# Loading one weight matrix in pieces over interleaved partitions, and the output in two stores

## The chip, the core and the metric

The kernel runs on one NeuronCore of a Trainium2 chip. The metric is the device time of one execution in microseconds (us). A profile of one execution shows what each engine did: TensorE (PE, with its weight loads PEld), VectorE (DVE), ScalarE (ACT), GpSimd (POOL), SyncE (SP, which issues most DMAs), and 16 DMA engines that all DMAs share.

## The reference

Two attention branches, A and B, take the same x (2 batches, one new token, 512 features). Each projects x to 32 heads of 128, attends over a cache of 4096 keys and values per head, and multiplies the result by output weights `wo` of 4096 x 512. A sigmoid gate mixes the branches. All is float32.

```python
g = sigmoid((x * gate_w).sum(-1, keepdims=True))
def branch(x, k, v, wq, wo):                      # k, v: (2, 32, 4096, 128)
    q = (x @ wq) as (2, 32, 1, 128)
    p = softmax(q @ k^T * 128 ** -0.5)
    return (p @ v) as (2, 1, 4096) @ wo
out = g * branch(A) + (1 - g) * branch(B)         # (2, 1, 512)
```

## The kernel before

The caches are read once, 512 MB of them, in 32 units: a unit is four heads of one batch of one branch (A's 16 units first, then B's). A K or V tile of a unit is 128 partitions x 64 KB: partition 32h + s holds positions 128s to 128s + 127 of head h of the four. Three buffers of 64 KB per partition carry all the large tiles: two named `kt` (K tiles, the query weights, the last unit's V and B's output weights) and one named `vt` (V tiles, and A's output weights at the end).

Per unit, `scores` (L158, L159) multiplies K by the query on VectorE and sums over the head dimension; `soft` (L164 to L172) finds the maximum on VectorE and takes the exponentials on ScalarE; `values` (L184) multiplies the probabilities with V on TensorE. The program order is written out by hand. All large loads are issued by SP and so wait in one queue: `load_k` (L65), `load_v` (L72), `load_wq` (L76), `load_wo` (L82 for A, L86 for B). A load that reuses a buffer waits at SP until the last reader of the buffer is done, and what SP issues later waits behind it.

At the end of the loop, unit 30 issues the last V (into a `kt` buffer) before its `values`, and A's output weights after it, since they take over the `vt` buffer that `values` reads. Unit 31 issues B's output weights after its scores are done. A's weights, 32 blocks of 512 columns per partition (64 KB, `NJ` = 32), come in one DMA over 128 partitions. B's come in six over 128 partitions, of 16, 8, 4, 2, 1 and 1 blocks (`TAIL`).

After the loop, `finish("B")` normalizes B's rows. TensorE then adds A's 32 and B's first 24 blocks into four strips of one PSUM tile (L252), ScalarE copies it (L255), four matmuls add up the strips (L259), and B's last eight blocks are added as they arrive (L262). VectorE copies the sum to `res` (L265), in which partition 32s + b holds columns 128s to 128s + 127 of batch b. Four stores of 2 partitions x 512 B write it out (L269), two issued by SP and two by ScalarE (ACT).

The small inputs, x (2 rows) and `gate_w` (1 row), are loaded by ScalarE's queue at the start (L90, L91).

Of the kernel before, what the change touches and what calls it, by code (L numbers as in the profile page):

```python
# [13 lines left out]
P = 128  # L14
B = 2
H = 32
SK = 4096
DH = 128
D = 512
KC = D // P  # L20
QP = 32
# [4 lines left out]
STRIPS = P // QP  # L26
HG = H // HU
HP = 2 * HU
NJ = D * H * DH // (P * D)
NB = 24  # L30
TAIL = ((0, 16), (16, 24), (24, 28), (28, 30), (30, 31), (31, 32))
PRW = QP + HU
# [5 lines left out]
def tile_gated_decode(ctx: ExitStack, tc: tile.TileContext, ins: dict, out: bass.AP):  # L38
    nc = tc.nc
# [12 lines left out]
    kt, vt, wq, wo = {}, {}, {}, {}  # L52
# [25 lines left out]
    def load_wo(n):  # L78
        src = ins[n + "_wo"].rearrange("(p j) e -> p j e", j=NJ)
        if n == "A":  # L80
            wo[n] = big.tile([P, NJ, D], F32, name="vt", bufs=1)
            nc.sync.dma_start(wo[n], src)  # L82
        else:
            wo[n] = big.tile([P, NJ, D], F32, name="kt")
            for i, j in TAIL:
                nc.sync.dma_start(wo[n][:, i:j], src[:, i:j])  # L86
# [63 lines left out]
    gat, rows = {}, {}  # L150
# [57 lines left out]
    def finish(n):  # L208
# [4 lines left out]
        nc.vector.tensor_tensor(r, r, rl[:, 1, :, None].to_broadcast([H, B, DH]), op=ALU.mult)  # L213
        t = ps.tile([P, B, NJ], F32, name="small")
        for q in range(HU):
            nc.tensor.matmul(t, deal[:, HU - 1 - q:HU - 1 - q + P], r[:, :, q * NJ:(q + 1) * NJ],  # L216
                             start=q == 0, stop=q == HU - 1)
        on[n] = work.tile([P, NJ, B], F32, name="on")
        nc.vector.tensor_copy(on[n].rearrange("p j b -> p b j"), t)
# [4 lines left out]
    for u in range(NU):  # L224
        scores(u)
        soft(u)
        if u == per_branch:
            finish("A")
        if u == per_branch - 2:
            load_wq("B")  # L230
        elif u == NU - 2:
            load_v(NU - 1)
        elif u == NU - 1:
            load_wo("B")
        else:
            load_k(u + 2 if u != per_branch - 1 else per_branch)
            if u == per_branch - 1:
                project("B")
                load_k(per_branch + 1)
        values(u)  # L240
        if u == NU - 2:
            load_wo("A")
        elif u < NU - 2:
            load_v(u + 1)
# [4 lines left out]
    for n in "AB":  # L249
        for j in range(NJ if n == "A" else NB):  # L250
            s = j % STRIPS
            nc.tensor.matmul(bulk[s * QP:s * QP + B], on[n][:, j], wo[n][:, j],  # L252
                             start=n == "A" and j < STRIPS, stop=n == "B" and j >= NB - STRIPS)
    bs = work.tile([P, D], F32, name="vs", bufs=1)
# [3 lines left out]
    for s in range(STRIPS):  # L258
        nc.tensor.matmul(acc[s * QP:s * QP + B], strip[:, :B], bs[:, s * DH:(s + 1) * DH], start=True, stop=False)  # L259
    for j in range(NB, NJ):  # L260
        for s in range(STRIPS):
            nc.tensor.matmul(acc[s * QP:s * QP + B], on["B"][:, j], wo["B"][:, j, s * DH:(s + 1) * DH],  # L262
                             start=False, stop=j == NJ - 1)
    res = consts.tile([P, DH], F32)
    nc.vector.tensor_copy(res, acc)  # L265
    dst = out.rearrange("b s e -> (b s) e")
    for s in range(STRIPS):
        eng = nc.sync if s % 2 == 0 else nc.scalar
        eng.dma_start(dst[:, s * DH:(s + 1) * DH], res[s * QP:s * QP + B])  # L269


# [20 lines left out]
```

## Time and profile before

| what | us |
|---|---|
| median of 3 runs | 1327.87 (1327.73 to 1327.96) |
| the profiled execution, whole | 1328.29 |
| its span, from the first to the last instruction | 1326.5 |
| VectorE busy | 1129.2 (85% of the span) |
| TensorE matmuls busy | 365.3 (28%) |
| ScalarE busy | 81.5 (6%) |

The mean granted TensorE clock of this execution was 0.645.

How to read the lines that follow. The queues of the page give packets, megabytes and the share of the 16 DMA engines' time; q1 is SP's queue, q10 ScalarE's, q8 and q14 bring instruction code. The chain is followed back from the last instruction to what released each step; in order of time it gives start, duration and what it was. The timeline gives start, duration, engine, line, operation, output<-input and count, with the idle time before in brackets and what ended it. The view by windows gives for a stretch, after its length, the busy time of PE, PEld, DVE, ACT and POOL with counts, then the granted clock, the mean busy share of the DMA engines and the GB/s they moved. A wait line gives who waited for what, the sum in us, how often, and the longest. A line's own view gives minimum, median and maximum duration in ns, and the first and last start in us.

### The profile page before, as it was taken

To read this page: it belongs to the slowest core of one execution; us is meant where nothing else is said; L and a number is where in the kernel's file an instruction comes from. 1 tells how busy PE (TensorE), PEld (TensorE's weight loads), DVE (VectorE), ACT (ScalarE), POOL (GpSimd) and SP (SyncE) were. 2 spreads that over 40 slices of the span, in tenths; PEclk is the share of its full clock that TensorE was granted. 3 is DMA by queue.
4 is the path that set the end of the run, shared out by engine and by line. 5 is a ranking of instruction groups with operands and counts; after the bars stand their busy time and mean duration, and the time that the engine had idled before them with its cause. 6 is when DMAs were issued, how large, how long until landed. Compare 5 with 4: busy or idle time off the path is not lost.

```text
span 1326.5 us, 5935 instructions
## 1 busy us (share of the span) xinstructions
PE 365.3 (28%) x2582; PEld 102.9 (8%) x2582; DVE 1129.2 (85%) x187; ACT 81.5 (6%) x283; POOL 1.8 (0%) x8
## 2 busy tenths in 40 slices
PE   3123113232321222231532122323212232320255
PEld 1000000000000000000111000000000000000011
DVE  1999988889988888998269999889888888988850
ACT  0000000000000000000000000000001000000000
POOL 0000000000000000000000000000000000000000
PEclk9666566666656666665865566666556666655678
DMA  9999999999999999999999999999999999999997
GB/s 411 441 413 441 441 435 423 437 441 419 441 435 439 425 439 431 437 433 427 433 440 435 433 435 428 441 435 429 431 441 437 425 435 439 437 421 439 441 432 317
DMA packets 10848, 570.82 MB, mean 430 GB/s; under 512 B 1211, under 2 KB 1219, under 8 KB 1606
## 3 DMA queue, kind: packets, MB, share of 16 engines
q1 hardware_dynamic: 10808, 570.43, 99.4%
q8 instruction: 20, 0.33, 0.1%
q14 instruction: 6, 0.05, 0.0%
q10 hardware_dynamic: 14, 0.01, 0.0%
HBM read 570.43 MB, written 0.00 MB: 430 GB/s over the span
## 4 chain that ended last, share of the span: by engine, by line
DVE 50%; DMA 49%; issue 0%; PE 0%; SPq 0%; DVEq 0%
DVE sc L159 25%; DVE kt L158 25%; DMA kt<-in_A_k_cache_dram 25%; DMA kt<-in_B_k_cache_dram 22%; DMA kt<-in_B_wo_dram 3%; PE small L216 0%; SPq L86 0%; DVE rm L164 0%; DVE tm L166 0%; DVE nm L168 0%; PE q L262 0%; DVE rows L213 0%; SPq L76 0%; DVEq L159 0%; DVE res L265 0%
## 5 line engine op out<-in xcount | busy, mean ns | idle before, releaser
L158 DVE TENSOR_TENSOR kt<-kt,q 128x16384 f32<-128x16384 f32 (+1 forms) x34 | 551.3, 16215 | 133.3 <-DMA kt<-in_B_k_cache_dram 71.8
L159 DVE TENSOR_REDUCE sc<-kt 128x128 f32<-128x16384 f32 (+1 forms) x34 | 551.3, 16216 | 3.2
L184 PE MATMUL vp<-vt,pr 128*32 128x512 f32 x1984 | 283.6, 736 | 856.6 <-DMA vt<-in_A_v_cache_dram 446.0
L184 PEld LDWEIGHTS vp<-vt,pr 128*32 128x32 f32 x1984 | 78.5, 132 | 1059.7 <-issue 1059.7
L172 ACT ACTIVATE pr<-sc,nm 32x128 f32<-32x128 f32 x128 | 66.2, 517 | 755.2 <-DVE nm L168 752.4
L144 PE MATMUL q<-kt,xb 128*32 128x512 f32 x256 | 30.8, 642 | 22.5 <-DMA kt<-in_B_wq_dram 12.0
L189 ACT ACTIVATE vs<-vp 128x512 f32<-128x512 f32 x16 | 9.6, 597 | 440.8 <-PE vp L184 440.8
L172 ACT ACTIVATION_READ_ACCUMULATOR pr<-sc,nm 32x1 f32 x128 | 25.2, 197 | 0.0
L193 PE MATMUL gat<-vs,strip 128*32 128x512 f32 x32 | 16.7, 605 | 11.4 <-ACT vs L189 11.4
L265 DVE COPY res<-q 128x128 f32<-128x128 f32 x1 | 0.3, 292 | 22.6 <-PE q L262 22.6
L210 DVE RECIPROCAL rl<-rows 32x2 f32<-32x2 f32 x2 | 0.3, 148 | 17.3 <-ACT rows L206 17.3
L216 PE MATMUL small<-rows,deal 32*128 32x64 f32 x16 | 3.0, 346 | 35.0 <-DVE rows L213 35.0
L184 PE MATMUL vp<-kt,pr 128*32 128x512 f32 x64 | 9.6, 770 | 10.4 <-DMA kt<-in_B_v_cache_dram 10.4
L144 PEld LDWEIGHTS q<-kt,xb 128*32 128x32 f32 x256 | 8.6, 118 | 43.9 <-issue 33.3
L164 DVE TENSOR_REDUCE rm<-sc 128x1 f32<-128x128 f32 x32 | 9.2, 286 | 1.1
L252 PE MATMUL q<-vt,on 128*2 128x512 f32 x64 | 8.5, 691 | 3.8 <-DMA vt<-in_A_wo_dram 3.8
L166 DVE STREAM_TRANSPOSE tm<-rm 128x32 f32<-128x32 f32 x32 | 6.8, 212 | 1.1
L118 DVE COPY xg<-small 128x12 f32<-128x12 f32 x1 | 0.2, 171 | 8.3 <-PE small L116 8.3
L168 DVE TENSOR_REDUCE nm<-tm 128x1 f32<-128x32 f32 x32 | 6.0, 186 | 1.1
L252 PE MATMUL q<-kt,on 128*2 128x512 f32 x48 | 5.5, 592 | 2.3 <-DMA kt<-in_B_wo_dram 2.3
L216 PEld LDWEIGHTS small<-rows,deal 32*128 32x128 f32 x16 | 2.7, 254 | 35.5 <-ACT pr L172 34.0
L203 PE MATMUL small<-vs,pick 128*32 128x128 f32 x32 | 4.2, 276 | 2.8 <-ACT vs L199 2.8
(44 smaller groups left out, 30.4 us busy)
## 6 DMA issues: line engine op xcount, KB each, us to landing
kt<-in_A_k_cache_dram SPq DMA_DIRECT2D x2, 4096.0 KB, 36.2
kt<-in_B_k_cache_dram SPq DMA_DIRECT2D x2, 4096.0 KB
kt<-in_B_wo_dram SPq DMA_DIRECT2D x1, 4096.0 KB
kt<-in_B_wo_dram SPq DMA_DIRECT2D x1, 2048.0 KB
kt<-in_B_wo_dram SPq DMA_DIRECT2D x1, 1024.0 KB, 39.8
kt<-in_B_wo_dram SPq DMA_DIRECT2D x1, 512.0 KB
kt<-in_B_wo_dram SPq DMA_DIRECT2D x2, 256.0 KB, 40.8
vt<-in_A_v_cache_dram SPq DMA_DIRECT2D x16, 29.3
```

The source lines that it names most:

```text
L144: nc.tensor.matmul(q[h * QP:(h + 1) * QP], xb[:, b, c, :], cols[:, c, h, half * HG // 2:(half + 1) * HG // 2, :], start=c == 0, stop=c == ...
L158: nc.vector.tensor_tensor(k, k, q[:, None, :].to_broadcast([P, j - i, DH]), op=ALU.mult)
L159: nc.vector.tensor_reduce(sc[u][:, i:j], k, axis=AX.X, op=ALU.add)
L164: nc.vector.tensor_reduce(rm[:, 0:1], sc[u], axis=AX.X, op=ALU.max)
L166: nc.vector.transpose(tm, rm[:, 0:1].to_broadcast([P, QP]))
L168: nc.vector.tensor_reduce(nm, tm, axis=AX.X, op=ALU.max, negate=True)
L172: nc.scalar.activation(w, sc[u][r].rearrange("p (c a) -> p c a", a=VC), AF.Exp, bias=nm[r], accum_out=lsum[r, g * HU + h:g * HU + h + 1])
L184: nc.tensor.matmul(o[s * QP:(s + 1) * QP], pr[:, c, at:at + QP], vt[u][:, c * VC:(c + 1) * VC, :].rearrange("p a d -> p (a d)"), start=not ...
L189: nc.scalar.activation(vs, o, AF.Copy)
L193: nc.tensor.matmul(gat[n, b][r:r + QP], strip, vs, start=True, stop=True)
L216: nc.tensor.matmul(t, deal[:, HU - 1 - q:HU - 1 - q + P], r[:, :, q * NJ:(q + 1) * NJ], start=q == 0, stop=q == HU - 1)
L252: nc.tensor.matmul(bulk[s * QP:s * QP + B], on[n][:, j], wo[n][:, j], start=n == "A" and j < STRIPS, stop=n == "B" and j >= NB - STRIPS)
```

## The change

A's output weights come in six DMAs, all issued by SP in the same place: blocks 0 to 7 over all 128 partitions, then blocks 8 to 31 (48 KB per partition) in five DMAs that each take some of the partitions: 0, 2, 4, ... (64 of them); 1, 5, 9, ... (32); 3, 11, 19, ... (16); 7, 15, ..., 63 (8); 71, 79, ..., 127 (8). Together they load what the one DMA loaded. The output is written by two stores, one of each batch's four pieces of 512 B, the first issued by SP and the second by ScalarE.

```diff
+NA = 8
...
         if n == "A":
             wo[n] = big.tile([P, NJ, D], F32, name="vt", bufs=1)
-            nc.sync.dma_start(wo[n], src)
+            nc.sync.dma_start(wo[n][:, :NA], src[:, :NA])
+            for rows in (slice(0, P, 2), slice(1, P, 4), slice(3, P, 8), slice(7, P // 2, 8), slice(P // 2 + 7, P, 8)):
+                nc.sync.dma_start(wo[n][rows, NA:], src[rows, NA:])
...
-    dst = out.rearrange("b s e -> (b s) e")
-    for s in range(STRIPS):
-        eng = nc.sync if s % 2 == 0 else nc.scalar
-        eng.dma_start(dst[:, s * DH:(s + 1) * DH], res[s * QP:s * QP + B])
+    dst = out.rearrange("b o (s e) -> b (o s) e", s=STRIPS)
+    src = res.rearrange("(s q) e -> q s e", q=QP)
+    nc.sync.dma_start(dst[0], src[0])
+    nc.scalar.dma_start(dst[1], src[1])
```

## The prediction

> **What bounds the kernel now.** I read the page first: queues, HBM rate and chain.
>
> ```profile
> span 1326.5 us, 5935 instructions
> q1 hardware_dynamic: 10808, 570.43, 99.4%
> q8 instruction: 20, 0.33, 0.1%
> q14 instruction: 6, 0.05, 0.0%
> q10 hardware_dynamic: 14, 0.01, 0.0%
> HBM read 570.43 MB, written 0.00 MB: 430 GB/s over the span
> DVE 50%; DMA 49%; issue 0%; PE 0%; SPq 0%; DVEq 0%
> ```
>
> The chain passes through VectorE and the DMAs in equal shares, but the busy DMA share of each stretch (second-last column of the view by windows) says which of the two waits for the other:
>
> ```profile
> 140.00:600.00 460.00, 118.61 (x790) 32.18 (x790) 420.69 (x57) 27.76 (x98) 0.00 (x0) 0.62 1.00 434
> 600.00:1280.00 680.00, 181.51 (x1260) 51.80 (x1260) 598.71 (x95) 42.04 (x149) 0.00 (x0) 0.64 1.00 433
> ```
>
> For 1140 us the engines of the DMA are never idle, at 434 and 433 GB/s. The bytes at that rate are the time; VectorE, 420.69 of 460 us busy, keeps up. The change moves the same bytes, so only the end counts. There I read the chain in order of time and the timeline:
>
> ```profile
> 1281.16 40.83 DMA kt<-in_B_wo_dram
> 1322.04 0.44 PE q L262 x8
> 1322.51 0.29 DVE res L265
> ```
>
> ```profile
> 1283.43 9.64 PE L184 MATMUL vp<-kt,pr 128*32 128x512 f32 x64 [10.44 <-DMA kt<-in_B_v_cache_dram]
> 1302.73 8.50 PE L252 MATMUL q<-vt,on 128*2 128x512 f32 x64 [3.82 <-DMA vt<-in_A_wo_dram]
> 1312.31 3.62 PE L252 MATMUL q<-kt,on 128*2 128x512 f32 x32 [1.07 <-DMA kt<-in_B_wo_dram]
> 1317.16 1.90 PE L252 MATMUL q<-kt,on 128*2 128x512 f32 x16 [1.24 <-DMA kt<-in_B_wo_dram]
> 1322.83 0.62 SPq L269 DMA_DIRECT2D out_dram<-res  x2
> 1322.83 0.83 ACTq L269 DMA_DIRECT2D out_dram<-res  x2
> ```
>
> The last V lands at 1283.4, A's output weights (8 MB) at 1302.7, the pieces of B's from 1312.3 on, the last at 1322.04. From there eight matmuls, one copy and the stores lead to the end. How evenly the 16 engines arrive there shows in half-microseconds:
>
> ```profile
> 1317.00:1317.50 0.50, 0.34 (x4) 0.11 (x8) 0.00 (x0) 0.00 (x0) 0.00 (x0) 1.00 0.80 328
> 1317.50:1318.00 0.50, 0.50 (x8) 0.10 (x4) 0.00 (x0) 0.00 (x0) 0.00 (x0) 1.00 0.75 307
> 1318.00:1318.50 0.50, 0.50 (x12) 0.10 (x4) 0.00 (x0) 0.00 (x0) 0.00 (x0) 1.00 0.55 225
> 1318.50:1319.00 0.50, 0.50 (x8) 0.00 (x0) 0.00 (x0) 0.00 (x0) 0.00 (x0) 1.00 0.54 217
> 1319.00:1319.50 0.50, 0.06 (x4) 0.00 (x0) 0.00 (x0) 0.32 (x1) 0.00 (x0) 1.00 0.50 197
> 1319.50:1320.00 0.50, 0.17 (x8) 0.17 (x12) 0.00 (x0) 0.28 (x1) 0.00 (x0) 1.00 0.54 213
> 1320.00:1320.50 0.50, 0.50 (x27) 0.48 (x23) 0.00 (x0) 0.00 (x0) 0.00 (x0) 1.00 0.36 127
> 1321.50:1322.04 0.54, 0.35 (x12) 0.06 (x8) 0.00 (x0) 0.00 (x0) 0.00 (x0) 1.00 0.02 8
> ```
>
> The share stands near one half for two microseconds: eight engines are through early (the last at about 1319.3, by the 0.50), eight late (1320 to 1322.04). Two more things: the rate per share does not rise when half of them are idle (225/0.55 = 409, 213/0.54 = 394 GB/s), so the limit belongs to each engine's own way and is not a pool; and one engine's pace is 433/16 = 27.1 GB/s.
>
> **How rows go to engines.** Queue q10 carries x (2 rows), the gate (1 row) and two stores of 2 rows: 7 data packets, yet it has 14. Queue q1 has 75 loads of 128 rows (34 of K, 32 of V, 2 of the query weights, 7 of the output weights) and two stores: 75 x (128 + 16) + 2 x (2 + 2) = 10808, exactly its count. So each row is a packet, and each engine that takes part adds one: 16 engines for 128 rows, 2 for 2 rows. A load of 8 rows thus runs on eight engines at most.
>
> **The change, part by part.**
>
> 1. Extra rows. 64, 32 and 16 rows give each engine 4 + 2 + 1 = 7 rows of 48 KB where it had 8; the two 8-row loads give 2 more to each of eight engines, if it is the same eight. Eight engines then carry 9 rows and eight carry 7. One row is 49152 B / 27.1 GB/s = 1.8 us. If the early eight get them, the late ones end at 1322.04 - 1.8 = 1320.2 and the early ones at 1319.3 + 1.8 = 1321.1: a gain of 0.9. If the late eight get them: 1.8 lost.
>
> 2. Pace of the small pieces. All 75 loads of before cover all 128 partitions; none of 16 or 8 rows, eight partitions apart, was timed. From below: such a row keeps the 1.8 us (no excess is possible the other way, since 27.1 GB/s is held everywhere). From above: if an engine's way ends in a group of partitions, rows eight apart load some groups from two engines and leave others empty, and each row takes twice as long: x = 1.8 us more. The receiving eight have three such rows (16, 8 and 8), the others one. The nearest row is the rate per share above: every way is full when the rows are spread evenly, and an idle neighbour lends nothing. I take the upper end: a full way that gets a second stream can only halve it. Then the receiving eight, if they are the early ones, end at 1319.3 + 1.8 + 3 x 1.8 = 1326.5, and the others at 1320.2 + 1.8 = 1322.0. Load term: 1326.5 - 1322.04 = +4.5.
>
> [...]
>
> Which eight receive? No view numbers the engines. The rows that bear on it:
>
> ```profile
> 1324.00:1324.50 0.50, 0.00 (x0) 0.00 (x0) 0.00 (x0) 0.00 (x0) 0.00 (x0) 1.00 0.04 17
> 1324.50:1325.00 0.50, 0.00 (x0) 0.00 (x0) 0.00 (x0) 0.00 (x0) 0.00 (x0) 1.00 0.01 2
> q14 instruction: 1, 0.01, 1.1%
> ```
>
> (the last from the DMA view of 1323.4 to 1325.2). The lateness must come from work that only some engines have, and q8's 20 code packets of 0.33 MB are the only such work of size: 2 or 3 each for eight engines, 16.5 KB or 0.6 us apiece at least. The last store traffic (1324.5 on) comes just after a q14 packet of 8 KB, as if stores of two rows shared engines with q14, which leaves q8 to the others. An 8-row load uses the engines of a 2-row transfer and six more, I assume. From this alone I put it at a little over 8 in 10 that the receiving eight are the early ones.
>
> [...]
>
> 3. More packets and waits: +0.1. Each engine has 15 or 17 rows for A's weights instead of 8, and 6 or 4 completion packets for one. B's last small pieces, 2 to 8 KB a row, ran at 394 to 409 GB/s per share against 433, up to 9% below; at 16 and 48 KB I take a tenth of that, under 1% of the 19.3 us of this load, with bounds of 0 and 0.5.
>
> 4. Issues and queues on SP.
>
> ```profile
> SPq L82 <- PE vp L184: 9.4, 1, 9.4
> SPq L86 <- DVE rm L164: 5.8, 1, 5.8
> SPq L269 <- DMA vt<-in_A_wo_dram: 21.0, 1, 21.0
> ```
>
> ```profile
> 1273.04 0.33 SPq L82 DMA_DIRECT2D vt<-in_A_wo_dram  x1
> 1278.90 2.70 SPq L86 DMA_DIRECT2D kt<-in_B_wo_dram  x6
> ```
>
> ```profile
> L252 PEldq EVENT_SEMAPHORE  x1: 51/51/51, 1302.6 to 1302.6; - x1
> ```
>
> A's load is issued at 1273.04, when the reader of V's buffer is done (the 9.4 us). Five more issues at 2.70/6 = 0.45 take 2.3 us and end at 1275.7. SP then waits for B's buffer until 1278.90 (the 5.8 us), which covers them; uncovered they would cost nothing either, as the last V still streams until 1283.4. The 21.0 us at L269 is a store that waits for A's weights although it doesn't use them: issues inherit the semaphore of one some eight earlier. With five loads put between, B's second piece will wait for V's landing (1283.4), and its third to sixth for A's first four pieces: 1288.2 (2 MB at 433), 1295.5, 1299.1, 1300.9. Behind the waiting SP stand only these pieces and the stores. Engines want the third piece at 1317.2, the early eight some 4 us sooner; 12 us of cover, cost 0. PE waits for six loads instead of one: five more waits of 51 ns, before 1302.7 and hidden. A's matmuls can start on the first quarter; 48 are left after the landing, 6.4 us instead of 8.50, so even a landing 4.5 later is done by 1313.6, ahead of B's first piece, which is later too. Cost 0.
>
> 5. The stores.
>
> ```profile
> L269 SPq DMA_DIRECT2D out_dram<-res x2: 257/289/321, 1322.8 to 1323.2; - x2
> L269 ACTq DMA_DIRECT2D out_dram<-res x2: 253/253/253, 1322.8 to 1323.4; - x2
> SPq L288 <- DMA out_dram<-res: 1.9, 1, 1.9
> ```
>
> Each queue issues one instead of two; the second started 0.4 (SP) and 0.6 (ACT) after the first. Those go for certain if landing takes as long: 0.4 is the lower end. The first pair's traffic is over by 1324.0, the second's falls after 1324.5; with the wait of 1.9 us for the last landing the upper end is 1.5. A store of 4 pieces of 512 B instead of 2 costs no more, on more engines. I take -0.9, nearer the middle, since the code packet may still be in the way.
>
> Sum: +4.5 + 0.1 - 0.9 = +3.7. The profiled execution took 1328.29 (1.8 around its span), 0.4 over the median of 1327.87: 1332.0 there, **1331.6** as a median.
>
> **The rivals.**
> - A: the small pieces keep their pace and the early eight get the rows: -0.9 + 0.1 - 0.9 = -1.7, **1326.2**; up to -1.8 + 0 - 1.5 = -3.3 if the early eight are done by 1318.4. Its point: with an excess x per row the sum is -1.7 + 3x, so under 0.6 us a row the change is not slower. For it: no narrow load is slow in any row. Against: idle ways lend nothing.
> - B: the late eight get the rows. With doubling 1322.04 + 1.8 + 5.4, +7.2 + 0.1 - 0.9 = +6.4, **1334.3**; without, +1.0. For it: no view numbers engines; against: the q14 packet among the stores.
> - C: the pieces are taken to overlap, as their partitions interleave, and each waits for the one before. Four waits of 0.45 (issue) plus some 0.7 (the stores are issued at 1322.83, traffic from 1323.5) add 4.6 with everything idle, and each 8-row load leaves eight engines idle for 1.8 us: +4.6 + 1.8 - 0.9, **1333.4**. For it: SP does inherit waits here; against: the partitions are disjoint.
> - D: the change does not shift anything, the two 8-row loads falling to different eights. Eight rows each; two of them doubled: +3.6 + 0.1 - 0.9, **1330.7**; without doubling 1327.1.
>
> **How the numbers follow.** Forecast 0.52, A 0.23, B 0.14, C 0.05, D 0.06. A measurement of this kernel tells about 0.2% from no change, 2.7 us: bounds 1325.2 and 1330.5. Faster: half of A, 0.12. Slower: of the forecast 0.44, the rest having x of 1.4 or less, B 0.12, C 0.05, D 0.03: 0.64. Same 0.24. The range runs from 1325.2 (A's better half left out) to 1335.2, B with its doubling inside; 0.17 is left out.
>
> **What would show it.** In the windows of 1290 to 1310, GB/s clearly under 420 with the DMA share still near 1 (doubled rows), or unchanged (A). At the end, a plateau of 0.5 that is later and ends later (forecast), gone (A), or twice as long (B). B's last landing at 1326.5, 1321.1 or 1329. Waits of SP at the line of A's pieces show C. The stores: one each, the end less than 3.9 us after the copy. The forecast is wrong above all if narrow loads keep 27.1 GB/s per engine.

## The result and the profile after

The changed kernel takes **1337.29 us** (median of 6 runs, 1335.37 to 1337.96); before, on the same chip, 1327.72 (6 runs, 1327.67 to 1327.96). The ratio is 1.0068, 95% interval 1.0058 to 1.0078: slower by 9.6 us where 3.7 were forecast, and above the range. The profiled execution took 1337.33.

The page after, span, queue and rate:

```profile
span 1335.5 us, 5939 instructions
q1 hardware_dynamic: 11000, 570.43, 99.3%
HBM read 570.43 MB, written 0.00 MB: 427 GB/s over the span
```

The bytes are the same; 192 packets more are 128 rows and 64 completion packets (4 x 16 + 2 x 8 for the six loads, less 16), so, at one completion packet an engine as counted in the prediction, the 8-row loads do run on eight engines each. The timeline after, in the order of time (line numbers are 3 higher than before):

```profile
1272.15 3.19 SPq L85 DMA_DIRECT2D vt<-in_A_wo_dram  x5
1298.84 3.59 PE L255 MATMUL q<-vt,on 128*2 128x512 f32 x16 [0.91 <-DVE q L251]
1312.76 7.56 PE L255 MATMUL q<-vt,on 128*2 128x512 f32 x48 [10.33 <-DMA vt<-in_A_wo_dram]
1321.95 3.61 PE L255 MATMUL q<-kt,on 128*2 128x512 f32 x32 [1.63 <-DMA kt<-in_B_wo_dram]
1326.80 1.90 PE L255 MATMUL q<-kt,on 128*2 128x512 f32 x16 [1.23 <-DMA kt<-in_B_wo_dram]
1331.69 0.40 PE L265 MATMUL q<-kt,on 128*2 128x128 f32 x8 [0.23 <-DMA kt<-in_B_wo_dram]
1332.16 0.29 DVE L268 COPY res<-q 128x128 f32<-128x128 f32 x1 [33.24 <-PE q L265]
1332.48 0.58 SPq L271 DMA_DIRECT2D out_dram<-res  x1
1332.49 0.63 ACTq L272 DMA_DIRECT2D out_dram<-res  x1
```

All of A's weights are there at 1312.76 instead of 1302.73, ten microseconds later, and every later piece stays that late: B's last lands at 1331.69 instead of 1322.04, +9.65. From there to the end it takes 3.81 us (1335.5 - 1331.69) instead of 4.46. So the whole loss arises before 1312.76 and it is one of loading. Where in that time, the windows of 5 us tell (last three columns: granted clock, DMA share, GB/s; a packet counts whole in the stretch in which it begins, so a share can pass 1). Before:

```profile
1293.00:1298.00 5.00, 2.33 (x18) 1.12 (x14) 0.72 (x3) 1.46 (x3) 0.00 (x0) 1.00 0.94 403
1298.00:1303.00 5.00, 1.18 (x12) 0.91 (x15) 0.85 (x3) 0.00 (x0) 0.00 (x0) 0.59 0.96 413
1303.00:1308.00 5.00, 5.00 (x36) 0.93 (x32) 0.00 (x0) 0.00 (x0) 0.00 (x0) 0.73 1.02 439
1308.00:1313.00 5.00, 3.93 (x40) 0.79 (x36) 0.00 (x0) 0.00 (x0) 0.00 (x0) 1.00 0.93 398
```

and after:

```profile
1288.00:1293.00 5.00, 4.29 (x40) 1.08 (x32) 0.00 (x0) 0.60 (x1) 0.00 (x0) 1.00 0.94 406
1293.00:1298.00 5.00, 2.98 (x17) 2.18 (x16) 0.75 (x4) 0.87 (x2) 0.00 (x0) 0.88 1.27 308
1298.00:1303.00 5.00, 3.59 (x16) 0.40 (x16) 0.82 (x3) 0.00 (x0) 0.00 (x0) 0.50 0.95 206
1303.00:1308.00 5.00, 0.00 (x0) 0.00 (x0) 0.00 (x0) 0.00 (x0) 0.00 (x0) 0.50 0.98 252
1308.00:1313.00 5.00, 0.24 (x4) 0.14 (x8) 0.00 (x0) 0.00 (x0) 0.00 (x0) 0.50 0.83 249
1313.00:1318.00 5.00, 5.00 (x28) 0.86 (x24) 0.00 (x0) 0.00 (x0) 0.00 (x0) 0.57 0.94 406
```

Read share and rate together: from 1298 to 1313, for 15 us, the engines are about as busy as before and move 50 to 63% of what they did. Had only the eight engines with doubled rows been slow, the rate would have been three quarters, some 320. Against the 427 of the span the four low windows lack 119, 221, 175 and 178 GB/s; times 5 us and over 427 that is **8.1 us of loading**, or 16 us at half pace. The other 1.5 us are not in them.

### The profile page after: what moved, and what is told of

It is laid out like the page before. It is cut to its first block, busy times and chain, and to the rows that moved or that the text cites. A ratio compares the mean times of both kernels' runs of the same rounds, so it can differ in the third digit from the quotient of the medians.

```text
span 1335.5 us, 5939 instructions
## 1 busy us (share of the span) xinstructions
PE 374.2 (28%) x2582; PEld 104.1 (8%) x2582; DVE 1129.2 (85%) x187; ACT 81.5 (6%) x283; POOL 1.8 (0%) x8
## 4 chain that ended last, share of the span: by engine, by line
DMA 76%; PE 23%; issue 0%; SPq 0%; DVE 0%
DMA vt<-in_A_v_cache_dram 36%; DMA vt<-in_B_v_cache_dram 34%; PE vp L187 22%; DMA vt<-in_A_wo_dram 2%; DMA kt<-in_B_wo_dram 2%; DMA kt<-in_A_wq_dram 2%; PE q L147 1%; SPq L85 0%; PE q L265 0%; SPq L83 0%; SPq L66 0%; DVE res L268 0%
## 5 line engine op out<-in xcount | busy, mean ns | idle before, releaser
L187 PE MATMUL vp<-vt,pr 128*32 128x512 f32 x1984 | 288.5, 746 | 851.1 <-DMA vt<-in_A_v_cache_dram 444.5
L255 PE MATMUL q<-vt,on 128*2 128x512 f32 x64 | 11.2, 858 | 11.2 <-DMA vt<-in_A_wo_dram 10.3
```

Of the source, the lines that this page charges most:

```text
L187: nc.tensor.matmul(o[s * QP:(s + 1) * QP], pr[:, c, at:at + QP], vt[u][:, c * VC:(c + 1) * VC, :].rearrange("p a d -> p (a d)"), start=not ...
```

## The experiments

The theory after this reading, called that of pairs below: two DMA engines whose rows end in one group of partitions halve each other (step 2 of the prediction). A group is the set of partitions that one engine alone writes in a load over all 128; that engine is the group's owner, and another that writes there a guest. That there are such groups, which partitions form one and which engine owns it is my assumption: no view and no packet record numbers the engines. So where I say below, or the expectations, that rows share a group or lie in their engines' own, it is the theory that says so; what the runs show is which rows were loaded, how long they took and at what rate. Its rivals: that the number of DMAs and waits costs; that loads of few rows are slow whatever their partitions; that the uneven rows cost (9 and 7 an engine). And, once the size was known: that one shared group holds up all 16 engines, not only the two that share it. Differences below are of medians, each against before on the same chip (1327.69 to 1327.87).

**The stores alone**, the loads as before.

> The loads of before with the two stores of after. From the start of the last eight matmuls to the end of the span it was 4.46 us before (1326.5 - 1322.04) and 3.81 after (1335.5 - 1331.69), so if the stores alone did that: 0.65 us faster than before, 0.4 to 0.9. If the stores only looked better after because the code packet came at another time, nothing: within 0.2 us of before.

1327.02 against 1327.87, -0.85; ratio 0.9995 (0.9986 to 1.0004), so not told from none by the clock alone. Its trace, page, timeline and waits:

```profile
span 1325.3 us, 5933 instructions
...
1321.60 0.40 PE L262 MATMUL q<-kt,on 128*2 128x128 f32 x8 [0.19 <-DMA kt<-in_B_wo_dram]
...
SPq L288 <- DMA out_dram<-res: 1.1, 1, 1.1
```

From the last matmuls to the end 3.70 us, 0.76 less than before; the wait for the last landing is 1.1 instead of 1.9. Its median is the lowest of all the kernels here, though not told from that of before.

**The loads alone**, with the four stores of before. All the runs that follow have these stores too.

> The six loads of after with the four stores of before. All theories put the loss on the loads and differ only on its kind: the last landing was 9.65 us later after (1331.69 against 1322.04), the stores gave back 0.65, so +9.6 to +10.3 over before. If loads and stores act on each other (other engines taking the stores), it would be off that by over 0.5 us.

1337.55, **+9.68**; ratio 1.0071 (1.0057 to 1.0085). Loads and stores don't act on each other as far as this can tell.

**Other pieces.** Each run changes the list of rows:

```diff
-for rows in (slice(0, P, 2), slice(1, P, 4), slice(3, P, 8), slice(7, P // 2, 8), slice(P // 2 + 7, P, 8)):
+for rows in (slice(0, P, 2), slice(1, P, 4), slice(3, P, 4)):                      # 64, 32, 32
+for rows in (slice(0, P, 2), slice(1, P, 4), slice(3, P, 8), slice(7, P, 8)):      # 64, 32, 16, 16
+for rows in (slice(0, P // 2), slice(P // 2, P)):                                  # halves
+for rows in (slice(0, P, 2), slice(1, P, 2)):                                      # even, odd
```

> The last three pieces (16, 8 and 8 rows, eight apart) made one of 32 rows, four apart; stores of before. Theory (two engines whose rows end in one group of partitions halve each other): 32 rows four apart spread over all groups like the other two pieces, each engine has eight rows, so +0 to +0.5. Rival that the number of DMAs, waits and completion packets costs: three more loads instead of five, so three fifths of some 10 us, +6. Rival that any load of fewer than 128 rows is slow: 56 of 64 KB... the same pieces of 64 and 32 rows and a third, +5 or more.

> The two loads of 8 rows made one of 16 rows, eight apart; stores of before. No engine has more rows than another. Theory of shared groups: two rows of every engine take twice the time, +3.6 if the pace of the others is not touched; after lost 10 with a forecast of 4.5 for its loads, so by the same ratio +8. Rival that the nine rows of eight engines make the loss (the imbalance): +0 to +0.5.

> Two pieces of 64 rows instead of the five: partitions 0 to 63, then 64 to 127; stores of before. Wide pieces, eight rows for each engine, but all 16 engines on one half of the partitions at a time. Theory of shared groups, if a group is a block of neighbouring partitions or of partitions eight apart within a half: every row of 48 KB takes twice the time as long as all engines are in the same piece, 8 x 1.8 = +14.4 at most, +7 or more. If groups cut across both halves, or if only pieces of few rows are slow: +0 to +0.5.

> As the run with two halves, but partitions 0, 2, 4, ... and then 1, 3, 5, ...; stores of before. The 64 rows two apart kept the pace in after, so +0 to +0.5 by every theory but one: that a load of fewer than 128 rows is slow whatever its partitions, which gives this run the time of the one with halves.

| pieces | us | against before | ratio (95%) |
|---|---|---|---|
| 64, 32, 32 | 1328.13 | +0.26 | 1.0005 (0.9996 to 1.0014) |
| 64, 32, 16, 16 | 1335.71 | +7.84 | 1.0061 (1.0046 to 1.0077) |
| halves | 1347.68 | +19.88 | 1.0147 (1.0132 to 1.0162) |
| even, odd | 1328.13 | +0.33 | 1.0004 (0.9995 to 1.0013) |

64 rows cost nothing that can be told two apart and 19.9 us side by side, over the 14.4 that I had as the most. It isn't the width of a load but which partitions it has. The windows of the run by halves, the first, one in the middle, and the last of the eight low ones, and the first after them:

```profile
1283.00:1288.00 5.00, 5.00 (x28) 1.39 (x32) 0.00 (x0) 0.00 (x0) 0.00 (x0) 0.56 1.26 279
...
1298.00:1303.00 5.00, 3.89 (x18) 0.51 (x17) 0.85 (x3) 0.00 (x0) 0.00 (x0) 0.50 1.14 239
...
1318.00:1323.00 5.00, 0.73 (x4) 0.11 (x8) 0.00 (x0) 0.00 (x0) 0.00 (x0) 0.50 0.83 321
1323.00:1328.00 5.00, 5.00 (x44) 1.11 (x40) 0.00 (x0) 0.00 (x0) 0.00 (x0) 0.81 0.99 426
```

With even and odd partitions, the stretch of the middle row:

```profile
1298.00:1303.00 5.00, 4.09 (x30) 1.06 (x33) 0.85 (x3) 0.00 (x0) 0.00 (x0) 0.66 1.05 455
```

Half the rate at full share, 239 against 455, with 64 rows a load in both: only the partitions differ. Why these are slow and those are not, the rates don't show.

The run with two pieces of 16 has eight rows for every engine, and yet costs 7.84: the imbalance is not the main thing. But nor does the bookkeeping of step 2 give it: two rows of each engine doubled would be 3.6. Its windows:

```profile
1293.00:1298.00 5.00, 2.81 (x19) 1.67 (x19) 0.72 (x3) 1.05 (x3) 0.00 (x0) 1.00 1.07 239
1298.00:1303.00 5.00, 3.66 (x20) 0.63 (x19) 0.85 (x3) 0.00 (x0) 0.00 (x0) 0.66 1.05 229
1303.00:1308.00 5.00, 0.00 (x0) 0.00 (x0) 0.00 (x0) 0.00 (x0) 0.00 (x0) 0.76 0.81 206
1308.00:1313.00 5.00, 3.28 (x20) 0.69 (x24) 0.00 (x0) 0.00 (x0) 0.00 (x0) 0.56 0.97 413
```

15 us at half pace, where two doubled rows last 7.2.

**Number of DMAs, and bytes in the pieces.** The first run has six loads over all partitions, the second the five pieces of the change with a third of their bytes (`NA = 24`):

```diff
-for rows in (slice(0, P, 2), ...):
-    nc.sync.dma_start(wo[n][rows, NA:], src[rows, NA:])
+for i, j in ((NA, 20), (20, 26), (26, 29), (29, 31), (31, NJ)):
+    nc.sync.dma_start(wo[n][:, i:j], src[:, i:j])
```

```diff
-NA = 8
+NA = 24
```

> Six loads for A's output weights as in after, of the same sizes in all (8, then 12, 6, 3, 2 and 1 blocks), but each over all 128 partitions; stores of before. It has the issues, the waits and the completion packets of after and none of its partitions. Theory of shared groups: +0 to +0.5. Rival that the number of DMAs and their waits costs: +8 to +10.

> The loads of after with 24 blocks in the first load instead of 8, so that the five pieces have rows of 16 KB instead of 48; stores of before. The same partitions, DMAs, packets and waits, a third of the bytes in the small pieces. Theory of shared groups: the loss goes by bytes, a third of some 10 us, +3.3 (2.5 to 4.5). A cost per DMA, per wait or per packet would stay at +8 to +10.

Six loads over all partitions: 1328.14, +0.34, ratio 1.0003 (0.9994 to 1.0013). SP waits in the same places, as often as in the change and somewhat shorter:

```profile
SPq L89 <- DMA vt<-in_A_wo_dram: 16.2, 4, 6.9
SPq L89 <- DMA kt<-in_B_v_cache_dram: 4.2, 1, 4.2
```

So issues, waits and completion packets cost nothing that can be told. A third of the bytes: 1331.98, +4.18, ratio 1.0029 (1.0017 to 1.0040); near the third of 9.68 (3.2), so the loss goes mostly by bytes.

**Rows loaded a second time.** To add one suspect at a time, these runs load 32, 64 and 32 rows, which by the theory share nothing (as pieces of 64, 32 and 32 they cost 0.26), and then some rows again:

```diff
+for rows in (slice(3, P, 4), slice(0, P, 2), slice(1, P, 4)):
+    nc.sync.dma_start(wo[n][rows, NA:], src[rows, NA:])
+nc.sync.dma_start(wo[n][3::8, NA:], src[3::8, NA:])          # 16 rows, eight apart
+nc.sync.dma_start(wo[n][3::4, 20:], src[3::4, 20:])          # or 32 rows of half the bytes
+nc.sync.dma_start(wo[n][3:32:4, NA:], src[3:32:4, NA:])      # or 3, 7, ..., 31
+nc.sync.dma_start(wo[n][67:96:4, NA:], src[67:96:4, NA:])    # or 67, 71, ..., 95
```

> Pieces of 32 (3, 7, 11, ...), 64 and 32 rows, and then 16 of the rows, 3, 11, 19, ..., a second time; stores of before. One row of 48 KB more for each engine, on groups that two engines share. If only the 16 rows pay: 1.8 us for the bytes and 1.8 for the half pace, 3.6 over the run of 64, 32 and 32 rows, +3.9 over before. If the rows beside them are slowed too: two such pieces cost 7.8 in the run with two of 16, so one costs 3.9 beside its bytes, +6 over before. If strided loads of 16 rows keep their pace: +2.1, as the next run.

> As the run before, but the second time all 32 rows 3, 7, 11, ... are loaded, with half the columns: the same bytes for each engine, and no group shared. Control for the bytes alone: one row more for each engine, 1.8, +2.1 over before by every theory.

> Eight rows a second time, 3, 7, ..., 31, by the eight engines that serve a load of eight rows; by the theory these rows lie in groups of these engines, so nothing is shared. It tells which eight they are. If the early ones: 1319.3 + 1.8 = 1321.1 is still before 1322.04, so as the run of 64, 32 and 32 rows, +0.3 (0 to +0.8). If the late ones: their 1322.04 moves by 1.8, +2.1.

> As the run before, with rows 67, 71, ..., 95: the same eight engines and bytes, the same distance between rows, but groups that by the theory belong to the other eight engines. If an engine's own time is the limit and groups are not: the time of the run before, +0.3 if these engines are the early ones. If only the displaced rows pay: the early ones end at 1319.3 + 1.8 + 1.8 = 1322.9, +1.2. If the owners of the groups lose the same time as the guests: the late ones end at 1322.04 + 1.8 at least, +2.1 or more. That is also the test of whether the early engines can take over work of the late ones at all.

| loaded again | us | against before | ratio (95%) |
|---|---|---|---|
| 16 rows, eight apart | 1336.01 | +8.30 | 1.0066 (1.0049 to 1.0083) |
| 32 rows, half the bytes | 1329.96 | +2.25 | 1.0016 (1.0007 to 1.0026) |
| 3, 7, ..., 31 | 1329.40 | +1.69 | 1.0015 (1.0005 to 1.0024) |
| 67, 71, ..., 95 | 1334.21 | +6.50 | 1.0048 (1.0033 to 1.0063) |

The bytes of a row more for each engine cost 2.0 (2.25 less 0.26), near the 1.8 of step 1. The same bytes eight apart cost 6.05 more than that, not 1.8, and the +8.30 is also over the +6 that I had if the rows beside them are slowed too. And the last two rows of the table, with as many bytes and the same distance of 4, and by the theory on the same eight engines, differ by 4.8 by which partitions they go to. Windows of the run with 3 to 31:

```profile
1298.00:1303.00 5.00, 4.09 (x26) 1.00 (x29) 0.85 (x3) 0.00 (x0) 0.00 (x0) 0.55 0.97 419
1303.00:1308.00 5.00, 5.00 (x44) 0.93 (x42) 0.00 (x0) 0.00 (x0) 0.00 (x0) 0.77 1.01 436
```

and with 67 to 95:

```profile
1298.00:1303.00 5.00, 3.72 (x17) 0.40 (x16) 0.85 (x3) 0.00 (x0) 0.00 (x0) 0.50 1.07 239
1303.00:1308.00 5.00, 0.81 (x5) 0.14 (x8) 0.00 (x0) 0.00 (x0) 0.00 (x0) 0.50 0.73 242
```

By the theory each guest shares here with one owner, 16 engines in all, so half pace of all of them could still be that of the pairs; but not for 9 us when a doubled row lasts 3.6. Two more runs set the theories apart, and one is a control for the first:

```diff
+nc.sync.dma_start(wo[n][67:72:4, NA:], src[67:72:4, NA:])    # 67 and 71
+nc.sync.dma_start(wo[n][3:64:8, NA:], src[3:64:8, NA:])      # or 3, 11, ..., 59
+nc.sync.dma_start(wo[n][3:8:4, NA:], src[3:8:4, NA:])        # or 3 and 7
```

> As the runs with eight rows a second time, but with two rows only, 67 and 71: two engines, and by the theory groups of two others. Theory of pairs: four of sixteen engines at half pace for some 4 us, the core at 7/8 of 427, 370 GB/s or more, and +0 to +2. Theory that sharing anywhere holds up every engine: the whole core at half pace, 215 to 250 GB/s, for 4 us or more, which is +2 or more over the run with two rows of the own half.

> As the runs with eight rows a second time, with rows 3, 11, ..., 59: eight engines, two to a group, all groups in the half of these engines. Theory of pairs: the other eight keep their pace, so the core runs at 3/4 of 427 or more, 320 GB/s, and the loss is that of the eight, 1.8 + 1.8 us less what they have in hand, +2 to +4. Theory that sharing anywhere holds up every engine: 215 to 250 GB/s for as long as in the run with rows 67, 71, ..., 95, and its +6.

> Rows 3 and 7 a second time: the same two engines as in the run with 67 and 71, in their own groups. Control for it: no fall of the rate, and +0 to +2 (1.8 us if one of the two is the last engine).

| loaded again | us | against before | ratio (95%) |
|---|---|---|---|
| 67 and 71 | 1329.83 | +2.14 | 1.0014 (1.0005 to 1.0024) |
| 3, 11, ..., 59 | 1333.55 | +5.86 | 1.0043 (1.0028 to 1.0058) |
| 3 and 7 | 1328.25 | +0.56 | 1.0004 (0.9995 to 1.0014) |

The windows of the run with 67 and 71:

```profile
1293.00:1298.00 5.00, 3.04 (x17) 1.91 (x14) 0.72 (x3) 0.86 (x2) 0.00 (x0) 0.88 1.04 436
1298.00:1303.00 5.00, 4.09 (x20) 1.05 (x20) 0.85 (x3) 0.00 (x0) 0.00 (x0) 0.50 0.91 275
1303.00:1308.00 5.00, 3.96 (x40) 0.98 (x40) 0.00 (x0) 0.00 (x0) 0.00 (x0) 0.94 1.02 439
```

with 3 and 7:

```profile
1298.00:1303.00 5.00, 3.27 (x20) 0.45 (x24) 0.13 (x1) 0.00 (x0) 0.00 (x0) 0.62 1.02 442
```

and with 3, 11, ..., 59:

```profile
1298.00:1303.00 5.00, 4.09 (x24) 1.44 (x23) 0.85 (x3) 0.00 (x0) 0.00 (x0) 0.53 1.07 229
1303.00:1308.00 5.00, 0.73 (x4) 0.00 (x1) 0.00 (x0) 0.00 (x0) 0.00 (x0) 0.50 0.75 223
```

That decides it. Two rows, four engines concerned by the theory of pairs: the rate would stay at 370 or more, and it falls to 275 over 5 us. With all engines at half pace for t of the 5 us, 427 x (1 - t/10) = 275 gives t = 3.6 us, just the time of one doubled row of 48 KB; the price, 1.58 over the control, is about half of that. By pairs alone it would take 14 us of sharing to lack as much. The trace's records of single packets, which no view above prints, say it directly: of the 13 rows that begin within two of these microseconds, all seven of 48 KB take 2.95 to 3.18 us instead of 1.815, and all six of 32 KB 1.92 to 2.45 instead of 1.213. Three rows of 48 KB that began up to a microsecond before and are still under way take 2.73 to 3.08, so these are 16 slow rows at once, as many as there are engines. In the change's trace it is the same: all 16 rows of 48 KB that begin between 1293.05 and 1294.4 take longer than 1.815 us (2.16 to 3.87), and the next 30, up to 1304.1, take 3.54 to 4.07. With 3, 11, ..., 59, by the theory shared within one half of the groups and eight engines concerned: 229 and 223, not 320. **In these runs two rows loaded again, 67 and 71, were enough to slow all 16 rows under way (48 KB in 2.73 to 3.18 us, 32 KB in 1.92 to 2.45), and 3 and 7 were not (442 GB/s).** That a shared group sets the two apart is the theory's reading; it fits every run here, and none shows it directly.

The packet records also give the loss of each engine, if its rows are followed from the end of one to the start of the next. In the change's trace each of the 16 takes 8.2 to 8.9 us more for its rows of 48 and 32 KB than 1.815 and 1.213 us a row, and the eight engines with seven rows of 48 KB lose as much as the eight with nine. With 67 to 95 each loses 4.2 to 4.9. Before, and in all eight runs that by the theory share no group, all rows of 16 KB or more that begin between 1282 and 1318 keep the time of their size, but for one, some 0.5 us longer. With halves each engine loses 18.1 to 20.0, over the 14.4 because the rows over all 128 partitions, just before and after the two halves, are slowed as well (by 3.6 on the mean).

What the low windows lack agrees with what the runs cost:

| run | lacking against 427 GB/s, us | cost, us |
|---|---|---|
| 67 and 71 again | 1.8 | 1.6 over 3 and 7 |
| 67 to 95 again | 4.4 | 4.8 over 3 to 31 |
| 3, 11, ..., 59 again | 4.7 | 4.2 over 3 to 31 |
| 64, 32, 16, 16 | 7.1 | 7.8 over before |
| the change's loads | 8.1 (trace of the change) | 9.7 over before |

**The rest of 1.5 us.** One run more, on which eight engines serve a load of 8 rows:

```diff
+for r in (3, 35):
+    nc.sync.dma_start(wo[n][r:r + 29:4, NA:], src[r:r + 29:4, NA:])
```

> As the run with rows 3, 7, ..., 31 a second time, and then 35, 39, ..., 63 as well, by the same eight engines and in their own groups: two rows of 48 KB more for each of them, nothing shared. If they are the early eight: 1319.3 + 3.6 = 1322.9, 0.9 behind the late ones, +1.2 over before. If late ones are among them: 3.6 later than the run of 64, 32 and 32 rows, +3.9.

1331.10, +3.36; ratio 1.0021 (1.0012 to 1.0030), which reaches from +1.6 to +4.0 and leaves +1.2 out. Over the run of 64, 32 and 32 rows, one row for the eight costs 1.4 and two cost 3.1: about 1.5 a row, so I read that engines that arrive late are among the eight. In its trace all rows of 48 KB but one keep 1.815 us, so this is the bytes alone. In the change's own loads the imbalance shows as the difference to the run of 64, 32, 16 and 16: 9.68 - 7.84 = 1.8. It closes the account, 8.1 + 1.5 to 1.8 against 9.65, though each of these differences is known to a microsecond or so only.

## Why the prediction was wrong, step by step

The direction was right, and so was the kind of the loss, rows that take twice as long by the partitions that are loaded. That shared groups are the cause fits every run, but no view shows a group. How far the slowdown reaches was wrong, and the forecast was 6 us short.

1. **Extra rows.** 1.8 us a row was right (2.0 measured). That the early eight get them was not: one and two rows more for each of eight engines, by the theory in their own groups, cost 1.4 and 3.1. Instead of a gain of 0.9 the imbalance cost 1.5 to 1.8. The packet records of the change's trace show why: eight engines are early and eight late, as I read, but of the eight with nine rows of 48 KB six begin them early (1282.9 to 1284.6) and two late (1286.8 and 1286.9). The last such row of these two ends at 1311.0 and 1311.4, those of all the others by 1307.8. My sign for it was a code packet among the stores, and the two rows of x; it was worth less than 8 in 10, and that an 8-row load uses the engines of a 2-row transfer was an assumption that no run shows. That the two 8-row loads fall to the same eight was right: nine rows on eight engines and seven on the others, and ten and eight in the run that loads 3 to 31 and 35 to 63 again. It is read from rows followed end to start, as the records don't number the engines.
2. **Pace: the step that failed.** "The receiving eight have three such rows (16, 8 and 8), the others one." The groups behind it were my assumption, and the doubled row my upper end: no row of before shows either. Doubling was right (2.95 to 3.18 us for 1.815 with 67 and 71 loaded again, mostly 3.6 and up to 4.1 in the change). The bookkeeping that charged it only to the engines with shared rows was not: with 67 and 71 the core's loading fell short by as much as half pace of all 16 engines for 3.6 us. For the change I had 8 x 3 and 8 x 1 doubled rows, 32 x 1.8 / 16 = 3.6 us of lost loading on the mean; the windows show 8.1, and the packet records 8.2 to 8.9 on every engine, also on those for which the prediction had one doubled row. The reading that misled me was that an idle neighbour lends nothing: at the end of before that holds (394 to 409 GB/s per share with about half of the engines idle, 433 with none), and it says nothing on what a busy one takes.
3. **More packets:** +0.1 forecast, 0.3 in the three runs with more loads that by the theory share no group, none told from zero.
4. **Issues and queues:** as forecast. After, SP waits like this:

```profile
SPq L89 <- DMA vt<-in_A_wo_dram: 22.3, 4, 7.4
SPq L89 <- DMA kt<-in_B_v_cache_dram: 3.7, 1, 3.7
```

```profile
L85 SPq DMA_DIRECT2D vt<-in_A_wo_dram x5: 579/582/667, 1272.1 to 1274.8; - x5
```

   B's second piece waits for V, the next four for A's pieces, and none of it costs anything that can be told (+0.34 with the same waits). The 48 matmuls took 7.56 us instead of 6.4: the granted clock was 0.50 in the windows from 1298 to 1313 and 0.57 in the next. They were done at 1320.3, still before B's first piece at 1321.95.
5. **Stores:** -0.9 forecast, -0.85 in the medians and 0.76 and 0.65 in the traces.

Of the rivals, **A** falls with the windows. **B** had the right eight, or some of them, but the same bookkeeping, so 1334.3 was 3.0 short. **C** falls: the five issues stand within 2.7 us at L85, with no wait between. **D** falls with the rows counted in step 1: both 8-row loads went to the same eight.

Why it lasts so long is argued, not shown: engines come to their shared row up to 5 us apart (1317 to 1322 at the end of before), so three doubled rows in turn, 10.8, and 5 us give some 16 us at half pace, as the change has, and 8.6 for one row, where 67 to 95 have 8.8. The runs with pieces of 16 last longer than that sum (14 against 12.2 for two), so it isn't the whole of it. Where in the chip all engines are held up, nothing here shows. And in every run here row p of the weights goes to partition p, so that the sharing lies in the partitions written and not in the addresses read is argued from assumed groups that fit, not tested by a run of its own.

## What to carry to other kernels

In this kernel six loads over all 128 partitions with fewer columns each (+0.34 us) and pieces of 64 or 32 rows two or four apart (+0.26 and +0.33) cost nothing that could be told; with two pieces of 16 rows eight apart the loads cost 7.84 more, with one of 16 and two of 8 rows 9.68, and halves of 64 rows side by side 19.88. So size pieces by columns first, and time a narrow set of partitions before relying on it. Rows loaded into partitions that by the theory belong to another, still streaming engine cost more here than their bytes: 67 to 95 loaded again cost 4.8 more than 3 to 31, and 67 and 71 alone 1.58 more than 3 and 7. And if a resource is shared, charge the slowdown to everyone until a run shows who is spared.

## What had not been expected

- The spread of the slowdown: with 67 and 71 loaded again, four engines concerned by the theory, the rate of the whole core was 275 GB/s over 5 us, where it was 442 with 3 and 7.
- The same 64 rows per load cost 0.33 us two apart and 19.88 side by side.
- The two 8-row loads fell, as I read the packet records, to eight engines of which two began their rows late (1286.8 and 1286.9), so extra rows there come on top: 1.4 us for one row each, 3.1 for two.
